# Feed-forward groups made of two sequence chunks of two batches, with a new emission order, in a fused linear-attention and SwiGLU kernel

## Chip, cores and metric

The kernel runs on one core of a Trainium2 chip. The metric is the device time of one execution in microseconds. A core has five engines with a queue of instructions each: TensorE (PE; its weight loads are shown as PEld), VectorE (DVE), ScalarE (ACT), GpSimd (POOL) and SyncE (SP), which here only issues DMAs. Engines run their own queues in order and wait for each other by semaphores.

## What is computed

Two steps follow each other. The first is a linear attention with a decaying state for 4 batches, 8 heads, a sequence of 768 and a head size of 48; the second is a root-mean-square norm and a SwiGLU feed-forward over the 3072 tokens with 384 features and 1536 hidden units.

```python
for t in range(S):
    cur = np.einsum('bhd,bhe->bhde', u[None] * kt, vt)
    y[:, :, t] = np.einsum('bhd,bhde->bhe', rt, state + cur)
    state = wt[:, :, :, None] * state + np.einsum('bhd,bhe->bhde', kt, vt)
...
xn = x / rms * rms_g
g = xn @ w_gate
silu = g * (1.0 / (1.0 + np.exp(-g)))
return silu * (xn @ w_val) @ w_out
```

Inputs and output are float32.

## The kernel before

The sequence is cut into six chunks of 128 positions. A unit of attention work is a chunk n of a batch j, written n.j. All 8 heads of one (n, j) are handled together: a tile has 128 positions in its partitions and 384 features. The state goes from chunk n to chunk n+1 of the same batch.

The attention of one (n, j) is a chain of small steps:

- load_r, load_k, load_v and load_w fetch the inputs, 192 KB each, from SyncE's queue. For chunks 0 and 1 one load_w.0.j fetches the decays of both (384 KB, L257); the others are at L244.
- ln (ScalarE) takes the logarithm of w; cs_mm (TensorE, L391 to L398) sums it along the chunk; exp_r and exp_k (ScalarE) turn the sums into factors; r_mul and k_mul multiply r and k by them (L440, L446); w_tot keeps the chunk's whole decay.
- rk_pe transposes both on TensorE (L469) and rk_tr copies the result out on ScalarE (L478); from chunk 2 on, rk_tr is a DMA transpose from SyncE's queue (L474).
- q_mm multiplies them (L487, L489), q_mask_e and q_mask_o apply the causal mask. For the odd heads VectorE does this (L502) in the pairs listed in ODD_DVE; otherwise ScalarE copies (q_copy_o) and GpSimd masks (L505).
- cast_v makes v bf16, on ScalarE for chunks 0 and 1 (L374). st_mm and st_new update the state (L515, L521, L522).
- bonus_mul (two GpSimd products, L452 and L453), bonus_sum (L457) and bonus_v (L462) make the term with u.
- y_mm (L532, L535) and x_add (L540) give the attention output. x_sq (L545), x_rstd and xn_mul (L558) norm it. For chunks 0 to 3, xn_pe transposes it on TensorE (L569) and xn_out writes it with the gain into the tile xnt (L580); for chunks 4 and 5, a DMA transpose (xn_tr, L563) and a gain on GpSimd (xn_gain, L586) do.

The feed-forward works on groups of 512 tokens. Group n has its own xnt tile of 384 features by 512 tokens. For each of 12 slices f of the hidden units, gate_mm.n.f and val_mm.n.f are three matmuls of 512 columns (L598), silu is on ScalarE (L231), h_mul on VectorE (L616). Then o_mm.n.j (L630) multiplies with the output weights, 12 matmuls for each of the four column blocks, o_out copies the result and out_dma stores it (L645). **Before, group n is chunk n of all four batches.**

The weights are loaded by GpSimd, which casts them: load_gv.g.h (L346) with h = 0 for gate and 1 for value, g = 0 for the slices f below 4 and g = 1 for the rest; load_wo (L352) for the output weights. Each stands at one place in GpSimd's order.

The order of the work is written out in ORDER, 1106 steps, and a loop at the end calls the function of each step, so that every engine's queue has its steps in that order. PSUM is shared out in the same order by three rings: "a" (two banks: cs_mm's sums, gate), "b" (two banks: the other sums, value) and "q" (four banks: all else). A step takes the bank whose last reader stands earliest. 48 steps warm.x.0 are matmuls on a tile of zeros whose result nobody reads (L369); they stand among the first steps.

Of the kernel before, what the change touches and what calls it, by code (L numbers as in the profile page):

```python
# [25 lines left out]
load_r.0.1 load_w.0.1 load_k.0.0 load_k.0.1 ln.0.1 warm.31.0 load_w.0.0 ln.0.0 warm.0.0 warm.13.0 warm.28.0  # L26
bonus_mul.0.1 bonus_sum.0.1 load_r.0.0 load_v.0.0 bonus_mul.0.0 load_w.0.2 load_w.0.3 warm.29.0 load_k.0.2 load_v.0.1
load_r.0.2 bonus_mul.0.2 load_r.0.3 load_v.0.3 load_v.0.2 bonus_v.0.1 load_r.1.3 load_k.1.0 cs_mm.0.1 exp_k.0.1
warm.10.0 warm.17.0 warm.33.0 warm.38.0 exp_r.0.1 r_mul.0.1 k_mul.0.1 bonus_sum.0.0 bonus_v.0.0 cs_mm.0.0 exp_r.0.0
ln.0.2 exp_k.0.0 cast_v.0.0 r_mul.0.0 k_mul.0.0 w_tot.0.0 warm.8.0 warm.16.0 warm.12.0 warm.4.0 warm.30.0 w_tot.0.1  # L30
rk_pe.0.1 warm.15.0 warm.14.0 load_k.0.3 bonus_mul.0.3 load_r.1.1 load_r.1.0 load_k.1.1 load_v.1.1 load_r.1.2 ln.0.3
load_k.1.3 warm.20.0 warm.37.0 warm.2.0 warm.22.0 warm.23.0 warm.5.0 warm.3.0 rk_pe.0.0 warm.24.0 load_gv.0.1
load_k.1.2 load_v.1.0 load_w.2.1 warm.25.0 load_v.1.2 load_w.2.0 load_v.1.3 load_r.2.1 load_r.2.0 load_w.2.2 warm.32.0
# [649 lines left out]
```

## Time and profile before

| | us |
|---|---|
| median of 3 runs | 203.21 (203.05 to 203.41) |
| span of the profiled execution, first to last instruction | 202.2 |
| median less that span | 1.0 |
| PE busy | 192.6 (95%) |
| PEld busy | 113.5 (56%) |
| DVE busy | 146.1 (72%) |
| ACT busy | 136.6 (68%) |
| POOL busy | 134.3 (66%) |
| first L598 matmul (val_mm.0.2) starts | 33.19 |
| last of the weight loads of gate (f of 4 and over) lands | 39.9 |
| last o_mm matmuls start | 198.1 |

The profiled execution's own time is known by its span alone; the 1.0 us between it and the median of the runs is what lies around it. "Busy" adds up the durations of an engine's instructions; matmuls overlap, so a TensorE that is busy all the time can still do its work faster or slower. The page also has a row for the TensorE clock that the throttle granted, full speed in all 40 slices. Idle time of an engine matters only where another, or the end, waits for it, and the chain of waits tells where that is.

### The profile page before, as it was taken

How to read it: one execution, taken by the hardware profiler on the slowest of the kernel's cores; microseconds unless marked ns; L12 is line 12 of the kernel's file. 1: busy time of each engine (PE TensorE's matmuls, PEld its weight loads, DVE VectorE, ACT ScalarE, POOL GpSimd, SP SyncE). 2: the span in 40 equal slices, each digit the busy share in tenths (PEclk: the TensorE clock that was granted, in tenths of full speed). 3: DMA queues.
4: the chain of work that ended last, by engine and by line, in shares of the span. 5: the costliest groups of instructions: out<-in, count | busy, mean ns of one | idle time of the engine just before them, and what ended most of it. 6: DMA issues, size and time to landing. Idle time of an engine off the chain costs nothing.

```text
span 202.2 us, 4444 instructions
## 1 busy us (share of the span) xinstructions
PE 192.6 (95%) x1600; PEld 113.5 (56%) x1600; DVE 146.1 (72%) x289; ACT 136.6 (68%) x278; POOL 134.3 (66%) x198
## 2 busy tenths in 40 slices
PE   1999988899999999999999999999999999999994
PEld 1564655455666555665556665555555555555562
DVE  6257796658999699987988889788878972146521
ACT  2577699688998557997566978679867764046300
POOL 6527599658789966899789898859898742400000
PEclk9999999999999999999999999999999999999999
DMA  6999999989999999958999978996184022103022
GB/s 152 243 244 177 209 182 202 202 161 201 199 192 221 196 179 238 225 133 194 177 231 245 206 171 195 216 241 134 24 192 112 15 68 71 45 3 117 0 97 99
DMA packets 121566, 32.41 MB, mean 160 GB/s; under 512 B 116420, under 2 KB 120392, under 8 KB 121544
## 3 DMA queue, kind: packets, MB, share of 16 engines
q1 hardware_dynamic: 119504, 28.58, 67.2%
q0 software_dynamic: 2032, 3.54, 9.7%
q8 instruction: 12, 0.20, 0.4%
q14 instruction: 10, 0.08, 0.1%
q10 hardware_dynamic: 8, 0.00, 0.0%
HBM read 25.96 MB, written 4.72 MB: 152 GB/s over the span
## 4 chain that ended last, share of the span: by engine, by line
PE 79%; SPq 8%; DMA 8%; POOL 2%; issue 1%; ACT 0%; POOLq 0%
PE ps_av L598 12%; PE ps_bu L598 12%; PE ps_bv L598 10%; PE ps_au L598 10%; PE ps_qx L630 8%; PE ps_qv L630 7%; SPq L244 7%; DMA wg_sb<-in_moe_w_gate_dram 6%; PE ps_qz L630 5%; PE ps_qu L630 3%; SPq L257 2%; DMA kt<-in_k_dram 2%; PE ps_qu L487 1%; PE ps_av L406 1%; PE ps_qu L515 1%
## 5 line engine op out<-in xcount | busy, mean ns | idle before, releaser
L630 PEld LDWEIGHTS <-ht 128*128 128x128 bf16 x300 | 28.3, 98 | 16.9
L231 ACT ACTIVATE sg<-ps_av 128x512 bf16<-128x512 f32 x38 | 22.7, 598 | 18.4 <-PE ps_av L598 16.8
L616 DVE TENSOR_TENSOR ht<-ps_bu,sg 128x512 bf16<-128x512 f32 x38 | 26.1, 686 | 11.7 <-PE ps_bu L598 8.4
L598 PEld LDWEIGHTS <-wg_sb 128*128 128x128 bf16 x216 | 22.8, 114 | 20.2 <-DMA wg_sb<-in_moe_w_gate_dram 2.1
L598 PEld LDWEIGHTS <-wv_sb 128*128 128x128 bf16 x216 | 23.2, 114 | 19.3 <-DVE xnt L580 0.2
L616 DVE TENSOR_TENSOR ht<-ps_bv,sg 128x512 bf16<-128x512 f32 x34 | 23.3, 686 | 12.2 <-PE ps_bv L598 8.8
L452 POOL TENSOR_TENSOR ruk<-rt,kt 128x384 f32<-128x384 f32 x24 | 24.0, 1000 | 11.1 <-DMA kt<-in_k_dram 6.0
L598 PE MATMUL ps_av<-xnt,wg_sb 128*128 128x512 bf16 x114 | 30.9, 380 | 0.4 <-DMA wg_sb<-in_moe_w_gate_dram 0.4
L231 ACT ACTIVATE sg<-ps_au 128x512 bf16<-128x512 f32 x34 | 20.4, 599 | 16.0 <-PE ps_au L598 14.6
L598 PE MATMUL ps_bu<-xnt,wv_sb 128*128 128x512 bf16 x114 | 30.9, 380 | 0.0
L598 PE MATMUL ps_au<-xnt,wg_sb 128*128 128x512 bf16 x102 | 27.7, 381 | 0.8 <-DMA wg_sb<-in_moe_w_gate_dram 0.8
L598 PE MATMUL ps_bv<-xnt,wv_sb 128*128 128x512 bf16 x102 | 27.7, 380 | 0.0
L453 POOL TENSOR_TENSOR ruk<-ruk,u_bc 128x384 f32<-128x384 f32 x24 | 23.9, 997 | 1.9
L462 POOL TENSOR_TENSOR ydiag<-vt,diag 128x384 f32<-128x384 f32 x24 | 19.7, 830 | 0.9 <-DVE diag L457 0.8
L446 POOL TENSOR_TENSOR rk<-kt,ek 128x384 bf16<-128x384 f32 x20 | 19.9, 1003 | 0.3 <-ACT ek L231 0.3
L505 POOL TENSOR_SCALAR_AFFINE_SELECT qts<-qts 128x512 bf16<-128x512 bf16 x20 | 12.5, 636 | 10.7 <-ACT qts L498 10.7
L630 PE MATMUL ps_qx<-wo_sb,ht 128*128 128x384 bf16 x96 | 16.9, 326 | 0.0
L630 PE MATMUL ps_qv<-wo_sb,ht 128*128 128x384 bf16 (+1 forms) x96 | 15.9, 316 | 0.0
L558 ACT ACTIVATE xn<-xb,rstd 128x384 bf16<-128x384 f32 x24 | 14.1, 608 | 1.2 <-POOL rstd L554 1.2
L457 DVE TENSOR_REDUCE diag<-ruk 128x8 f32<-128x384 f32 x24 | 12.9, 543 | 2.7 <-POOL ruk L453 2.7
L231 ACT ACTIVATE lw<-wt 128x384 bf16<-128x384 f32 (+1 forms) x20 | 11.2, 579 | 4.6 <-DMA wt<-in_w_dram 4.5
L229 ACT ACT_TABLE_LOAD x10 | 12.8, 1283 | 1.8 <-PEq L667 1.6
(153 smaller groups left out, 368.2 us busy)
## 6 DMA issues: line engine op xcount, KB each, us to landing
rt<-in_r_dram SPq DMA_DIRECT2D x24, 192.0 KB, 3.9
kt<-in_k_dram SPq DMA_DIRECT2D x24, 192.0 KB, 3.9
vt<-in_v_dram SPq DMA_DIRECT2D x24, 192.0 KB, 3.7
out_dram<-ob SPq DMA_DIRECT2D x23, 192.0 KB, 2.1
wt<-in_w_dram SPq DMA_DIRECT2D x16, 192.0 KB, 3.9
wt<-in_w_dram SPq DMA_DIRECT2D x4, 384.0 KB, 4.6
wo_sb<-in_moe_w_out_dram POOLq DMA_DIRECT2D x3, 384.0 KB, 5.2
wg_sb<-in_moe_w_gate_dram POOLq DMA_DIRECT2D x1, 768.0 KB, 12.0
```

The lines of the kernel that those rows point to most:

```text
L229: nc.scalar.preload_act_table_set(table_name)
L231: return nc.scalar.activation(**kw).ins
L244: dmas["load_" + which, n, j] = nc.sync.dma_start(out=inp[which, n, j], in_=t[j, :, n * L:(n + 1) * L, :].rearrange("h t d -> t h d")).ins
L446: eng.tensor_tensor(out=rk[:, n % 2, j, 1, :, 0:D], in0=inp["k", n, j], in1=bank["cs_k", n, j][:, 0:DM].rearrange("p (h d) -> p h d", h=H) ...
L452: nc.gpsimd.tensor_tensor(out=ruk[n, j], in0=inp["r", n, j], in1=inp["k", n, j], op=ALU.mult)
L453: nc.gpsimd.tensor_tensor(out=ruk[n, j], in0=ruk[n, j], in1=u_bc, op=ALU.mult)
L457: nc.vector.tensor_reduce(out=diag[n, j].rearrange("p h o -> p (h o)"), in_=ruk[n, j], axis=mybir.AxisListType.X, op=ALU.add)
L462: nc.gpsimd.tensor_tensor(out=ydiag[n, j], in0=inp["v", n, j], in1=diag[n, j].to_broadcast([128, H, D]), op=ALU.mult)
L558: nc.scalar.activation(out=xn, in_=xb[n, j], func=AF.Copy, scale=rstd[n, j][:, 1:2])
L598: nc.tensor.matmul(ps, lhsT=units(ws, c, f), rhs=xnt[n][:, c, :], start=(c == 0), stop=(c == KC - 1))
L616: nc.vector.tensor_tensor(out=ht[n][:, f, :], in0=bank.pop(("v", n, f)), in1=bank.pop(("sg", n, f)), op=ALU.mult)
L630: nc.tensor.matmul(ps[:, cols], lhsT=ht[n][:, f, b * L:(b + 1) * L], rhs=wo_sb[:, f, cols], start=(f == 0), stop=(f == FC - 1))
```

## The change

The number of feed-forward groups and their size stay. Groups 0 and 1 get other columns: group 0 is chunks 0 and 1 of batches 0 and 1, group 1 chunks 0 and 1 of batches 2 and 3. COL maps an (n, j) to its group and column block, CHUNK maps back; x_cols gives the part of xnt to write, out_dma takes the rows from CHUNK. Groups 2 to 5 are as before. The four (n, j) whose k_mul, q_mask_o and x_rstd are on VectorE or ScalarE change with the groups: K_POOL, EXPK_SB, ODD_DVE and RSTD_ACT now list 0.0, 0.1, 1.0 and 1.1 where 0.0 to 0.3 stood, so q_copy_o.0.2 and q_copy_o.0.3 are there and q_copy_o.1.0 and q_copy_o.1.1 are not. xn_gain loses a branch that no step took. The rest of ORDER, to the last step, is written anew; it has the same number of steps. Its core, and the rest of the diff:

```diff
 ORDER = """
-load_r.0.1 load_w.0.1 load_k.0.0 load_k.0.1 ln.0.1 warm.31.0 load_w.0.0 ln.0.0 warm.0.0 warm.13.0 warm.28.0
-bonus_mul.0.1 bonus_sum.0.1 load_r.0.0 load_v.0.0 bonus_mul.0.0 load_w.0.2 load_w.0.3 warm.29.0 load_k.0.2 load_v.0.1
-load_r.0.2 bonus_mul.0.2 load_r.0.3 load_v.0.3 load_v.0.2 bonus_v.0.1 load_r.1.3 load_k.1.0 cs_mm.0.1 exp_k.0.1
-warm.10.0 warm.17.0 warm.33.0 warm.38.0 exp_r.0.1 r_mul.0.1 k_mul.0.1 bonus_sum.0.0 bonus_v.0.0 cs_mm.0.0 exp_r.0.0
-ln.0.2 exp_k.0.0 cast_v.0.0 r_mul.0.0 k_mul.0.0 w_tot.0.0 warm.8.0 warm.16.0 warm.12.0 warm.4.0 warm.30.0 w_tot.0.1
-rk_pe.0.1 warm.15.0 warm.14.0 load_k.0.3 bonus_mul.0.3 load_r.1.1 load_r.1.0 load_k.1.1 load_v.1.1 load_r.1.2 ln.0.3
...
-xn_mul.0.3 exp_k.1.3 xn_pe.0.3 r_mul.1.3 xn_out.0.3 cast_v.1.1 k_mul.1.1 load_gv.1.1 rk_pe.1.1 st_mm.1.1 exp_k.1.2
-exp_r.1.2 w_tot.1.2 r_mul.1.2 w_tot.1.3 bonus_mul.1.3 val_mm.0.2 val_mm.0.3 warm.46.0 gate_mm.0.2 gate_mm.0.3 rk_tr.1.1
-q_mm.1.1 silu.0.2 h_mul.0.2 load_k.2.0 silu.0.3 h_mul.0.3 bonus_sum.1.3 st_new.1.1 gate_mm.0.0 val_mm.0.1 rk_tr.1.0
-bonus_mul.1.0 val_mm.0.0 load_r.2.3 silu.0.0 q_mask_e.1.1 h_mul.0.0 bonus_mul.1.1 bonus_sum.1.1 gate_mm.0.6 silu.0.6
-gate_mm.0.1 silu.0.1 q_mm.1.0 q_copy_o.1.0 gate_mm.0.5 silu.0.5 h_mul.0.1 q_mask_e.1.0 bonus_sum.1.0 gate_mm.0.7
...
-gate_mm.4.10 silu.4.10 val_mm.4.10 h_mul.4.10 val_mm.4.11 h_mul.4.11 o_mm.4.1 o_mm.4.0 o_mm.4.2 x_rstd.5.2 xn_mul.5.2
-x_rstd.5.3 xn_mul.5.3 xn_tr.5.3 xn_tr.5.2 xn_gain.5.2 xn_gain.5.3 out_dma.3.3 xn_gain.5.1 o_mm.4.3 gate_mm.5.5 silu.5.5
-o_out.4.2 val_mm.5.5 gate_mm.5.2 h_mul.5.5 val_mm.5.2 gate_mm.5.1 silu.5.2 h_mul.5.2 silu.5.1 gate_mm.5.7 silu.5.7
...
+load_w.0.0 load_r.0.1 load_k.0.0 load_v.0.0 ln.0.0 warm.43.0 warm.24.0 warm.27.0 warm.20.0 warm.17.0 warm.25.0
+load_w.0.3 load_r.0.0 warm.9.0 warm.28.0 warm.22.0 warm.16.0 warm.30.0 warm.7.0 warm.34.0 warm.31.0 warm.5.0
+load_k.0.1 warm.19.0 warm.29.0 warm.42.0 warm.11.0 warm.15.0 warm.37.0 warm.47.0 warm.14.0 warm.39.0 cast_v.0.0
+load_w.0.1 ln.0.1 ln.0.3 warm.8.0 load_v.0.1 load_v.1.1 cast_v.1.1 warm.38.0 load_w.0.2 warm.13.0 warm.36.0 load_v.0.3
+load_r.1.1 load_k.1.1 ln.0.2 bonus_mul.0.1 bonus_sum.0.1 bonus_v.0.1 bonus_mul.0.0 warm.35.0 warm.21.0 warm.4.0
+warm.45.0 warm.46.0 warm.44.0 warm.0.0 warm.26.0 warm.32.0 warm.18.0 warm.6.0 warm.3.0 warm.10.0 warm.23.0 warm.12.0
+warm.33.0 bonus_sum.0.0 cast_v.0.1 cs_mm.0.1 warm.2.0 exp_r.0.1 cs_mm.0.0 exp_k.0.1 load_v.1.0 r_mul.0.1 exp_k.0.0
+k_mul.0.1 w_tot.0.1 k_mul.0.0 warm.41.0 warm.40.0 warm.1.0 rk_pe.0.1 exp_r.0.0 st_mm.0.1 st_mm.0.0 r_mul.0.0 w_tot.0.0
...
+k_mul.1.1 r_mul.1.1 rk_pe.1.1 q_mask_o.0.0 w_tot.1.1 load_k.1.3 load_k.1.2 load_k.0.2 load_r.0.2 load_gv.0.1
+bonus_v.0.0 cast_v.1.0 rk_tr.1.0 q_mm.1.0 exp_r.0.3 rk_tr.1.1 exp_k.0.3 cs_mm.0.2 exp_r.0.2 x_sq.0.1 q_mask_e.0.0
+q_mask_e.1.0 q_mask_o.1.0 y_mm.0.0 x_add.0.0 load_r.1.2 q_mm.1.1 load_v.0.2 q_mask_e.1.1 bonus_sum.1.0 q_mask_o.1.1
+w_tot.0.2 r_mul.0.3 x_sq.0.0 x_rstd.0.1 st_mm.1.0 y_mm.1.0 st_mm.1.1 load_v.1.3 load_v.1.2 load_gv.0.0 bonus_mul.0.3
+bonus_v.1.1 bonus_v.1.0 x_rstd.0.0 xn_mul.0.1 xn_mul.0.0 exp_k.0.2 y_mm.1.1 k_mul.0.3 w_tot.0.3 x_add.1.1 x_sq.1.1
+load_gv.1.0 k_mul.0.2 bonus_mul.0.2 x_add.1.0 load_w.2.0 load_w.2.1 xn_pe.0.1 load_r.2.0 load_w.2.2 load_r.2.1
...
+xn_mul.1.1 cs_mm.1.2 xn_pe.1.1 xn_mul.1.0 xn_pe.1.0 xn_out.1.1 exp_r.1.3 exp_k.1.2 exp_r.1.2 exp_k.1.3 xn_out.1.0
+rk_pe.0.2 st_mm.0.3 r_mul.1.3 w_tot.1.2 rk_tr.0.3 val_mm.0.2 st_new.0.3 k_mul.1.3 load_gv.1.1 k_mul.1.2 bonus_mul.1.3
+r_mul.1.2 w_tot.1.3 val_mm.0.3 st_new.1.1 gate_mm.0.3 silu.0.3 gate_mm.0.2 silu.0.2 q_mm.0.3 rk_pe.1.3 h_mul.0.3
+gate_mm.0.1 q_copy_o.0.3 cast_v.0.2 gate_mm.0.0 st_mm.0.2 val_mm.0.1 rk_tr.0.2 bonus_sum.0.3 q_mask_e.0.3 h_mul.0.2
+bonus_v.0.3 silu.0.1 silu.0.0 q_mm.0.2 val_mm.0.0 q_copy_o.0.2 bonus_sum.0.2 q_mask_o.0.2 gate_mm.0.5 bonus_v.0.2
+h_mul.0.1 q_mask_e.0.2 gate_mm.0.6 y_mm.0.2 silu.0.5 q_mask_o.0.3 gate_mm.0.7 st_new.0.2 h_mul.0.0 silu.0.6 silu.0.7
...
+silu.4.10 out_dma.3.3 xn_tr.5.0 xn_tr.5.1 x_sq.5.2 xn_mul.5.3 x_rstd.5.2 xn_mul.5.2 xn_tr.5.3 xn_gain.5.0 xn_tr.5.2
+val_mm.4.10 xn_gain.5.1 xn_gain.5.3 h_mul.4.10 h_mul.4.11 o_mm.4.1 o_mm.4.0 xn_gain.5.2 o_mm.4.2 out_dma.3.0
+out_dma.3.2 val_mm.5.2 gate_mm.5.2 gate_mm.5.8 val_mm.5.8 silu.5.2 silu.5.8 h_mul.5.2 gate_mm.5.1 silu.5.1 val_mm.5.1
...
 """
...
@@ -177,8 +178,8 @@
 
     CAST_ACT = sel("00 01 02 03 10 11 12 13")
     EXPR_SB = sel("")
-    K_POOL = sel("10 11 12 13 20 21 22 23 30 31 32 33 40 41 42 43 50 51 52 53")
-    EXPK_SB = sel("10 11 12 13") | K_POOL
+    K_POOL = sel("02 03 12 13 20 21 22 23 30 31 32 33 40 41 42 43 50 51 52 53")
+    EXPK_SB = sel("10 11") | K_POOL
     WIN = (0, 1)
     Q_PAIR = ((2, 0), (2, 2), (3, 0), (3, 2), (4, 0), (4, 2), (5, 0), (5, 2))
     OLD_DVE = (1, 2, 3, 4)
@@ -187,9 +188,15 @@
     GAIN_POOL = (4, 5)
     RK_PE = sel("00 01 02 03 10 11 12 13")
     RK_DVE = sel("")
-    ODD_DVE = sel("00 01 02 03")
-    RSTD_ACT = sel("00 01 02 03")
+    ODD_DVE = sel("00 01 10 11")
+    RSTD_ACT = sel("00 01 10 11")
     OUT_DVE = sel("00 02 10 12 20 22 30 32 40 42 50 52 53")
+
+    COL = {(0, 2): (1, 0), (0, 3): (1, 1), (1, 0): (0, 2), (1, 1): (0, 3)}
+    CHUNK = {v: k for k, v in COL.items()}
+
+    def col_of(n, j):
+        return COL.get((n, j), (n, j))
 
     def banks_of(fn, n, j):
         if fn == "q_mm":
@@ -337,7 +344,7 @@
     FG = 4
     wg_sb = [persist.tile([128, KC, (b - a) * 128], BF16, name="wg_sb%d" % a) for a, b in zip(GV, GV[1:])]
     wv_sb = [persist.tile([128, KC, (b - a) * 128], BF16, name="wv_sb%d" % a) for a, b in zip(GV, GV[1:])]
-    GV_BEHIND = (None, None)
+    GV_BEHIND = (None, None, None)
     WO_BEHIND = (None, None, None)
 
     def load_gv(g, h):
@@ -557,10 +564,14 @@
         xn = bank["xn", n, j] = pt.tile([128, DM], BF16, name="xn", bufs=3)
         nc.scalar.activation(out=xn, in_=xb[n, j], func=AF.Copy, scale=rstd[n, j][:, 1:2])
 
+    def x_cols(n, j):
+        g, c = col_of(n, j)
+        if g not in xnt:
+            xnt[g] = pt.tile([128, KC * TS], BF16, name="xnt")
+        return xnt[g].rearrange("p (c x) -> p c x", c=KC)[:, :, c * L:(c + 1) * L]
+
     def xn_tr(n, j):
-        if n not in xnt:
-            xnt[n] = pt.tile([128, KC, TS], BF16, name="xnt")
-        nc.sync.dma_start_transpose(xnt[n][:, :, j * L:(j + 1) * L], bank.pop(("xn", n, j)))
+        nc.sync.dma_start_transpose(x_cols(n, j), bank.pop(("xn", n, j)))
 
     def xn_pe(n, j):
         ps = bank["xt", n, j] = psum("q", ("xt", n, j), [128, KC, 128], BF16)
@@ -569,24 +580,19 @@
             nc.tensor.transpose(ps[:, c, :], xn[:, c * 128:(c + 1) * 128], ident)
 
     def xn_out(n, j):
-        if n not in xnt:
-            xnt[n] = pt.tile([128, KC, TS], BF16, name="xnt")
+        x_t = x_cols(n, j)
         ps = bank.pop(("xt", n, j))
         if (n, j) in XOUT_ACT:
             for c in range(KC):
-                nc.scalar.activation(out=xnt[n][:, c, j * L:(j + 1) * L], in_=ps[:, c, :], func=AF.Copy,
+                nc.scalar.activation(out=x_t[:, c, :], in_=ps[:, c, :], func=AF.Copy,
                                      scale=gT[:, c:c + 1])
         else:
-            nc.vector.tensor_tensor(out=xnt[n][:, :, j * L:(j + 1) * L], in0=ps,
+            nc.vector.tensor_tensor(out=x_t, in0=ps,
                                     in1=gT.to_broadcast([128, KC, L]), op=ALU.mult)
 
     def xn_gain(n, c):
-        if n in GAIN_POOL:
-            x = xnt[n][:, :, c * L:(c + 1) * L]
-            nc.gpsimd.tensor_tensor(out=x, in0=x, in1=gT.to_broadcast([128, KC, L]), op=ALU.mult)
-        else:
-            nc.vector.tensor_scalar(out=xnt[n][:, c, :], in0=xnt[n][:, c, :], scalar1=gT[:, c:c + 1],
-                                    scalar2=None, op0=ALU.mult)
+        x = x_cols(*CHUNK.get((n, c), (n, c)))
+        nc.gpsimd.tensor_tensor(out=x, in0=x, in1=gT.to_broadcast([128, KC, L]), op=ALU.mult)
 
     def units(ws, c, f):
         g = max(i for i, x in enumerate(GV) if x <= f)
@@ -595,7 +601,7 @@
 
     def fc_mm(ps, ws, n, f):
         for c in range(KC):
-            nc.tensor.matmul(ps, lhsT=units(ws, c, f), rhs=xnt[n][:, c, :],
+            nc.tensor.matmul(ps, lhsT=units(ws, c, f), rhs=xnt[n].rearrange("p (c x) -> p c x", c=KC)[:, c, :],
                              start=(c == 0), stop=(c == KC - 1))
 
     def gate_mm(n, f):
@@ -640,9 +646,11 @@
         bank["ob", n, j] = ob
 
     def out_dma(n, j):
+        ob = ("ob", n, j)
         b, cols = out_cols(n, j)
-        row0 = b * S + n * L
-        nc.sync.dma_start(out=out[row0:row0 + L, cols], in_=bank.pop(("ob", n, j))[:, cols])
+        i, j = CHUNK.get((n, b), (n, b))
+        row0 = j * S + i * L
+        nc.sync.dma_start(out=out[row0:row0 + L, cols], in_=bank.pop(ob)[:, cols])
 
 
     fns = locals()
```

## The prediction

> **What bounds the kernel now.** I read the page's summary, then the chain of waits that ended last, then its pieces in order of time. By engine the chain is nearly all TensorE:
>
> ```profile
> PE 79%; SPq 8%; DMA 8%; POOL 2%; issue 1%; ACT 0%; POOLq 0%
> ```
>
> The 21% that are not TensorE all lie ahead of 39.9 us. The chain in order of time (start, duration, what; the loads on SyncE's queue come before it):
>
> ```profile
> 18.64 3.76 DMA kt<-in_k_dram
> 22.47 1.00 POOL ruk L452
> 24.49 0.99 POOL wv_sb L346
> 26.34 0.78 issue
> 27.12 0.78 POOL ydiag L462
> 27.90 11.95 DMA wg_sb<-in_moe_w_gate_dram
> 39.90 0.84 PE ps_av L598 x3
> ```
>
> So: the loads, one after another; the last load of chunk 0 (k of batch 3) lands at 22.4; GpSimd makes the bonus product of it, and only then issues the weight loads that stand behind it in its order; the third of them, the gate weights for f of 4 and over, lands at 39.9. From there TensorE has no hole. The busy times by stretch (PE in the second column of figures) say the same:
>
> ```profile
> 30.00:35.00 5.00, 4.81 (x52) 2.94 (x50) 3.79 (x10) 4.95 (x13) 4.82 (x6) 1.00 1.21 206
> 35.00:40.00 5.00, 3.98 (x24) 1.88 (x25) 2.82 (x6) 3.54 (x5) 3.48 (x4) 1.00 1.13 201
> 40.00:45.00 5.00, 5.00 (x42) 2.91 (x43) 3.41 (x7) 3.63 (x7) 2.41 (x4) 1.00 0.90 172
> 80.00:90.00 10.00, 10.00 (x97) 6.33 (x94) 9.97 (x21) 9.19 (x22) 8.18 (x14) 1.00 0.84 187
> ```
>
> I checked it by counting. Matmul spacings from the timeline, warm clock: a gate or value unit 0.648 us, an o_mm 1.95 (the halves 0.99), cs_mm of the window 0.84, later 0.26 and 0.16, rk_pe 0.45, q_mm 0.33 a chunk, st_mm 0.165, xn_pe 0.165, y_mm 0.2 for chunk 0 and 0.4 later. Over the whole order this is 177 us. Ahead of gate_mm.0.6 (39.90) stand 17.9, behind it 159.4, and the last matmul ends about 199.3: 199.3 - 39.9 = 159.4. **After 39.9 there is nothing to win**, only to lose; ahead of it 39.9 us hold 17.9 us of work.
>
> **The sum's frame.** The new order has the same matmuls. Its time is 203.2 plus what the dense stretch starts later or earlier (each measured after crediting the work already done), plus new holes. The span was 202.2, the median of the runs 203.21; I put the 1.0 between them around the span, in both kernels.
>
> **Loads.** Counted in KB in SyncE's order, the last load that the first four chains need is number 18 in both: load_k.0.3 before, load_r.1.0 now, each at 4224 KB in all (the four 384 KB w loads are still among the first eleven). The queue never paused up to there (the pieces on it abut from 0.80 to 19.6 us), so load_r.1.0 lands at 22.4 too. The saving that the grouping allows, two w loads of 384 KB, isn't taken.
>
> **Warm matmuls.** 44 of the 48 now stand ahead of the first cs_mm, five before. They are spaced 0.32 us until 11.4 and 0.163 after: 17 of them from 5.94, then 27 x 0.163 = 4.4, so cs_mm.0.1 starts at about 15.8 instead of 7.5. Its w is the 2112th KB, whose Ln ran at 11.8 before, so some 3 us are lost to them. Covered: both chunks' cs_mm are through by about 22, when the load for r_mul.1.0 lands; if that cover goes, up to 1 us.
>
> **GpSimd up to the first unit.** From 22.47: bonus_mul.1.0 2.0, load_gv.0.1 at 24.5, bonus_v.0.0, load_gv.0.0 at 26.3, all as before. Then, where before one bonus_v (0.78) ended at 27.9, now come bonus_mul.0.3 (2.0), bonus_v.1.1 and bonus_v.1.0 (0.8 each): end 27.1 + 3.6 = 30.7, **2.8 later**. VectorE's own work is ready then (q_mask_o.1.1 about 29.0). The last x_add before started at 28.73, the first unit at 33.19: 4.46 of x_sq, rstd, xn_mul, transpose, xn_out. Now x_add.1.0 at 30.8 gives the first unit at 35.3.
>
> **From there to the dense stretch.** Ahead of gate_mm.0.5, the first that needs the late gate weights, stand 8 units 5.2, two q_mm 0.66, rk_pe 0.45, st_mm 0.17: 6.5, so 41.8; ScalarE's chain (four Exp 1.55, rkT copy 0.92, table load 1.28, Silu 0.52 each, from 34.2) lets it go at 42.0. Before, 39.90 with 17.9 us of work done; now 19.9 done (one rk_pe, q_mm, st_mm and unit more, and two y_mm of chunk 1 in place of chunk 0's). Even would be 41.9. **+0.1 to +0.2.**
>
> **Weight loads.** load_gv.1.0 is issued at 31.7 instead of 27.9, load_gv.1.1 at 36.7 instead of 30.6, behind k_mul and bonus_mul. Before, they landed one behind another at 32.0, 35.6, 39.9, 44.1. The third needs 4.3 after the second, so issued at 31.7 it lands at 39.9 to 41, the fourth at 44 to 45.5, and their first users are at 42.0 and 46.5. Cost 0; without that cover up to 1.
>
> **A wait that is new.** st_mm.0.2 stands in TensorE's order ahead of val_mm.0.1 and needs cast_v.0.2, hence load_v.0.2, load 26, at 5760 KB. Load 26 before (v of chunk 1, batch 0) was starved:
>
> ```profile
> 25.64 1.30 SPq L244 DMA_DIRECT2D vt<-in_v_dram  x1
> ```
>
> It took 15.1 us and landed at 40.7. The reason, in the DMA view from 36 to 38 us (packets, MB, share of the engines):
>
> ```profile
> q0 software_dynamic: 193, 0.37, 97.1%
> q1 hardware_dynamic: 195, 0.04, 16.4%
> ```
>
> Packets of the weight queue and of SyncE's queue alternate one for one, and a weight packet is some ten times as large. Behind the waiting cast_v.0.2 on ScalarE are rk_tr.0.2 and two Silu; on TensorE val, q_mm, val and gate. ScalarE reaches the cast at 39.5. At 40.7 the whole goes 1.1 later; with a landing before 39.5 it is free. GpSimd issues the third weight load 3.8 later, and from issue to first packets took some 2 us (24.5 to between 26 and 28), so SyncE's packets get a pause between the second and third: I take a landing near 38.6, cost 0: midway between 40.7 and the 36.6 at which SyncE's packets, summed over the DMA views, reached 5760 KB before.
>
> **Groups 1 to 4.** From the last y_mm of a group to its first unit TensorE has 11.2, 10.7, 14.0, 10.2 us of other work, before 10.9, 10.7, 7.8, 9.7: no worse. VectorE, ScalarE and GpSimd have as much work in all (k_mul, q_mask_o and rstd change chunks, not number), so I put 0.
>
> **Group 5.** Before, the first unit comes after all four o_mm of group 4; now after three. The cover from y_mm.5.2 to the first unit falls from 13.4 to 10.8. It was thin:
>
> ```profile
> 172.85 2.39 POOL L586 TENSOR_TENSOR xnt<-xnt,gT 128x384 bf16<-128x384 bf16 x3 [4.56 <-DMA xnt<-xn]
> ```
>
> The last gain ends at 175.24, the unit starts at 175.75. The new chain is shorter, for x_add.5.2 waits for one h_mul: x_add at 1.4 after y_mm.5.2 starts, second x_sq done at 4.95, rstd 5.8, xn_mul 6.4, the second transpose issued at 6.8, landed 2.7 to 3.7 later, gain 0.83: 10.3 to 11.4 against 10.8. I take **+0.6**; ends 0 and 2.1 (the old chain's length under the new cover).
>
> The x_cols views, the output rows and the unused third entry of GV_BEHIND add no instruction: 0, both ways.
>
> **Sum:** 203.2 + 0.2 + 0.6 = **204.0**.
>
> **Rivals.**
> *Earlier (faster), 202.5.* The place is x_add.1.0. If GpSimd's and VectorE's pieces overlap better than I laid them and the first unit starts at 34.4 or before, gate_mm.0.5 runs at 41.0, 0.9 ahead of even, with group 5 late by 0.2. It decides at 35.2 for the first unit. For it: the weights themselves land by 39.9 to 41. Against: GpSimd's order is fixed behind a load that lands at 22.4. 0.22.
> *The v wait bites, 205.1.* The 40.7 row as it stands: +1.1. 0.16.
> *Group 5 waits in full, or q_mm waits for transposes behind loads on SyncE's queue, 205.5.* The old chain under the new cover: 203.2 + 0.2 + 2.1. Against: the shorter steps above. 0.14.
> *The slow matmul spacing returns, 206.5.* These are two warm matmuls and the rate they started from:
>
> ```profile
> 9.97 0.52 PE L369 MATMUL ps_qx<-zero 128*128 128x384 bf16 x1
> ...
> 11.40 0.32 PE L369 MATMUL ps_qz<-zero 128*128 128x384 bf16 x1
> 11.56 0.33 PE L369 MATMUL ps_qu<-zero 128*128 128x384 bf16 x1
> ```
>
> It took 5.4 us of steady matmuls to halve the spacing. With warm matmuls gone after 18 us, TensorE works some 3.6 of the 5.8 us from 29.5 to 35.3; were it slowed again, the first 5.4 us of units would lose half, 2.7, less 0.2 hidden by the weights' landing. Against: no hole over about 1 us by my reckoning. 0.10. The Trainium skill ("TensorE: Matmul & The Clock Gate", What's actually happening and Part 4: PE-mode transpose) halves the clock after an idle window of about 3.4 us and doesn't count transposes as busy in the same way. That speaks against this order, for by my reckoning only transposes run from 33.0 to 35.3; but 2.3 us are less than that window, so by the rule the time stays at the forecast. No trace here shows the clock fall back.
>
> **Chances.** Forecast 0.38, the rivals as given. About 0.2% (0.4 us) is what a measurement can tell from no change. Faster 0.22; same 0.14 (the lower part of the forecast); slower 0.64. Range 202.3 to 206.0: it leaves out the slowest rival and the far end of the first.
>
> **What would show it.** The first L598 matmul at 35.3 (33.2 before); first use of the late gate weights near 42.0; cast_v.0.2 not waiting for its load; a hole under 1 us ahead of group 5's first unit; none elsewhere after 42. It is wrong if the first unit comes before 34.5, if spacings of 0.43 us (twice 0.216) for 128x512 matmuls appear, or if waits appear in groups 1 to 4.

## The result and the profile after

The changed kernel takes **209.13 us** (median of 4 runs, 207.81 to 210.28), the kernel before 203.13 beside it: a ratio of 1.028 (1.023 to 1.034), 6 us slower. (Ratios are the record's own estimate and can differ a little from that of two medians; they leave out the longest run of three kernels further down, a2, w1 and w3, which the record counts as slow.) The forecast was 204.0, the range 202.3 to 206.0. The profiled execution is the 207.81 one, with a span of 206.1 us.

The chain by engine, where before had 79% TensorE:

```profile
PE 57%; SPq 12%; POOL 11%; DMA 7%; ACT 5%; issue 3%; DVE 2%; POOLq 0%; DVEq 0%; ACTq 0%
```

The chain now leaves TensorE in the middle of the kernel. There are three kinds of loss.

**Holes.** A hole here is the time from one matmul's start to the next beyond its streaming, counted from 0.25 us up (the profile's idle time is some 0.15 shorter, for it ends at the modelled end). Behind the first feed-forward group before had none. The changed kernel has 0.26 at 92.16, 0.56 at 126.88, 0.27 at 129.81, 1.48 at 135.38, 0.52 at 153.00: **3.1 us**. (One more, 0.31 at 47.22, lies in its first group and is counted with the start.) The largest two, from TensorE's timeline (start, duration, engine, line, tile; in brackets the idle time and what ended it):

```profile
126.88 0.23 PE L494 MATMUL ps_qx<-rkT 48*128 48x128 bf16 x1 [0.39 <-DMA rkT<-rk]
...
135.38 0.23 PE L494 MATMUL ps_qz<-rkT 48*128 48x128 bf16 x1 [1.32 <-DMA rkT<-rk]
```

Both are q_mm of chunk 4, waiting for a transpose from SyncE's queue. The one at 153.00 is the first unit of group 4, waiting for the gain that GpSimd applies behind the last transpose of its tile.

**A sparse start.** TensorE's timeline some microseconds ahead of the first unit:

```profile
27.82 0.33 PE L522 MATMUL ps_qv<-vb,rk 128*128 128x96 bf16 x4
28.88 0.33 PE L539 MATMUL ps_qu<-st,rkT 128*128 128x96 bf16 x4 [0.73 <-DVE qts L509]
29.04 0.36 PE L542 MATMUL ps_qu<-vb,qts 128*128 128x48 bf16 x8
30.73 0.33 PE L580 MATMUL ps_qu<-ident,xn 128*128 128x128 bf16 x3 [1.33 <-DVE xb L547]
```

From 28.0 to 30.7 it does 0.4 us of work. In this execution that costs nothing: the clock stays up, the first unit starts at 35.25 and the first late gate weights are used at 41.93. In three of the four runs the mean granted clock is 0.989 to 0.991 instead of 1.000, and they take 209.03 to 210.28. The experiments show what happens there.

**The ends.** Time less span is 1.7 us in every run of both kernels (207.81 less 206.1); from the last matmul's end to the span's end it is 3.3 us, before 2.95.

### The profile page after: what moved, and what is told of

Its sections match the earlier page's. It is cut to its first block, busy times and chain, and to the rows that moved or that the text cites. A ratio compares the mean times of both kernels' runs of the same rounds, so it can differ in the third digit from the quotient of the medians.

```text
span 206.1 us, 4427 instructions
## 1 busy us (share of the span) xinstructions
PE 191.3 (93%) x1580; PEld 114.2 (55%) x1600; DVE 146.0 (71%) x289; ACT 136.9 (66%) x278; POOL 135.1 (66%) x198
## 3 DMA queue, kind: packets, MB, share of 16 engines
HBM read 25.96 MB, written 4.72 MB: 149 GB/s over the span
## 4 chain that ended last, share of the span: by engine, by line
PE 57%; SPq 12%; POOL 11%; DMA 7%; ACT 5%; issue 3%; DVE 2%; POOLq 0%; DVEq 0%; ACTq 0%
PE ps_av L604 10%; PE ps_bv L604 10%; SPq L251 9%; PE ps_au L604 8%; PE ps_bu L604 8%; PE ps_qz L636 4%; PE ps_qx L636 4%; PE ps_qu L636 4%; PE ps_qv L636 3%; SPq L264 3%; POOL ruk L459 2%; POOL ruk L460 2%; DMA rkT<-rk 2%; DMA kt<-in_k_dram 2%; DMA wt<-in_w_dram 2%
## 5 line engine op out<-in xcount | busy, mean ns | idle before, releaser
L622 DVE TENSOR_TENSOR ht<-ps_bv,sg 128x512 bf16<-128x512 f32 x39 | 26.8, 687 | 20.2 <-PE ps_bv L604 11.1
L238 ACT ACTIVATE sg<-ps_av 128x512 bf16<-128x512 f32 x39 | 23.4, 599 | 21.4 <-PE ps_av L604 17.6
L604 PE MATMUL ps_bv<-xnt,wv_sb 128*128 128x512 bf16 x109 | 31.0, 380 | 0.3
L238 ACT ACTIVATE sg<-ps_au 128x512 bf16<-128x512 f32 x33 | 19.8, 600 | 13.3 <-PE ps_au L604 9.2
L622 DVE TENSOR_TENSOR ht<-ps_bu,sg 128x512 bf16<-128x512 f32 x33 | 22.7, 688 | 8.4 <-PE ps_bu L604 5.2
L604 PE MATMUL ps_bu<-xnt,wv_sb 128*128 128x512 bf16 x95 | 26.4, 380 | 0.5 <-POOL xnt L595 0.4
L604 PE MATMUL ps_au<-xnt,wg_sb 128*128 128x512 bf16 x95 | 26.3, 380 | 0.3
L460 POOL TENSOR_TENSOR ruk<-ruk,u_bc 128x384 f32<-128x384 f32 x24 | 24.4, 1015 | 1.9
L636 PE MATMUL ps_qu<-wo_sb,ht 128*128 128x384 bf16 x96 | 16.9, 326 | 0.0
L552 ACT ACTIVATE junk<-xb 128x384 bf16<-128x384 f32 x24 | 12.5, 521 | 1.2 <-DVE xb L547 1.0
```

The costliest lines, as they stand in the source:

```text
L238: return nc.scalar.activation(**kw).ins
L460: nc.gpsimd.tensor_tensor(out=ruk[n, j], in0=ruk[n, j], in1=u_bc, op=ALU.mult)
L604: nc.tensor.matmul(ps, lhsT=units(ws, c, f), rhs=xnt[n].rearrange("p (c x) -> p c x", c=KC)[:, c, :], start=(c == 0), stop=(c == KC - 1))
L622: nc.vector.tensor_tensor(out=ht[n][:, f, :], in0=bank.pop(("v", n, f)), in1=bank.pop(("sg", n, f)), op=ALU.mult)
L636: nc.tensor.matmul(ps[:, cols], lhsT=ht[n][:, f, b * L:(b + 1) * L], rhs=wo_sb[:, f, cols], start=(f == 0), stop=(f == FC - 1))
```

## The experiments

All kernels in one table, but for x1 and y1, which come under "The queue". "Clock held": runs with a mean granted clock of 0.998 or more. (One stretch of 3.41 us at half speed takes 0.008 off the mean, so the 0.997 of one run each of w3 and e2 is less than one such stretch. The profiles of e1 and z1 hold no clock record; there the spacing of the matmuls shows no fall.) The profile's columns: its run's time, the start of the first unit, the holes behind the first group, and the "rest", the end of the last matmul less the holes; it shows what the start costs, for the matmuls of the groups are the same. Ratios are to the kernel before, with their 95% interval.

| kernel | median, us | ratio | clock held | run | first unit | holes | rest |
|---|---|---|---|---|---|---|---|
| before | 203.1 | | all | | 33.19 | 0 | 199.3 |
| before, again | 204.00 | | 1 of 1 | 204.00 | 33.57 | 0.9 | 198.5 |
| changed | 209.13 | 1.028 (1.023 to 1.034) | 1 of 4 | 207.81 | 35.25 | 3.1 | 199.7 |
| changed, again | 209.79 | 1.034 (1.028 to 1.040) | 1 of 4 | 209.85 | 37.26 | 3.2 | 201.6 |
| changed, third | 210.74 | 1.034 (1.029 to 1.039) | 0 of 6 | 211.21 | 38.16 | 3.7 | 202.4 |
| e1 transposes first | 208.31 | 1.025 (1.018 to 1.032) | 3 of 4 | 206.80 | 35.91 | 1.6 | 200.5 |
| h1 new start, old rest | 208.26 | 1.025 (1.018 to 1.032) | 1 of 4 | 206.69 | 35.47 | 1.4 | 200.2 |
| h2 old start, new rest | 209.80 | 1.034 (1.028 to 1.040) | 0 of 4 | 209.84 | 33.66 | 4.4 | 200.8 |
| w1 filled | 208.67 | 1.027 (1.024 to 1.031) | 5 of 6 | 208.05 | 36.09 | 2.5 | 200.5 |
| w2 fewer first warms | 209.46 | 1.031 (1.028 to 1.034) | 0 of 6 | 209.06 | 36.77 | 2.8 | 201.2 |
| w3 both | 211.15 | 1.035 (1.030 to 1.040) | 2 of 6 | 211.25 | 37.72 | 3.9 | 202.3 |
| w4 h1, filled | 207.52 | 1.021 (1.018 to 1.024) | 5 of 5 | 207.76 | 36.75 | 1.4 | 201.3 |
| w5 h1, fill in one bank | 206.67 | 1.019 (1.017 to 1.021) | 4 of 4 | 206.49 | 35.19 | 1.7 | 199.7 |
| w6 changed, fill in one bank | 206.11 | 1.016 (1.012 to 1.019) | 6 of 6 | 207.61 | 35.97 | 2.3 | 200.3 |
| e2 w6, loads behind | 205.76 | 1.016 (1.013 to 1.018) | 5 of 6 | 205.48 | 35.36 | 0.7 | 199.7 |
| z2 e2, more loads behind | 207.73 | 1.022 (1.019 to 1.026) | 6 of 6 | 207.57 | 35.78 | 2.1 | 200.5 |
| z1 before, loads behind | 206.69 | 1.017 (1.013 to 1.022) | 4 of 6 | 206.25 | 33.71 | 3.1 | 198.5 |
| b2 before, fewer late warms | 203.35 | 1.000 (0.998 to 1.003) | 1 of 12 | 202.01 | 32.62 | 0 | 197.3 |

### Which half, and does it repeat

Four kernels ran first: the changed kernel unedited (a1); e1, with the transposes of chunk 4 ahead in SyncE's queue; and two mixed orders, cut at the first unit of group 2.

```diff
 e1:
-... rk_tr.4.0 out_dma.2.1 out_dma.1.3 load_v.4.2 rk_tr.4.1 load_v.4.3 load_v.5.3 ... rk_tr.4.3 rk_tr.4.2
+... rk_tr.4.0 rk_tr.4.1 out_dma.2.1 out_dma.1.3 load_v.4.2 load_v.4.3 rk_tr.4.3 rk_tr.4.2 load_v.5.3 ...
 h1: changed order up to gate_mm.2.5, then the steps that are left in before's order
 h2: before's order and code up to val_mm.2.1, then the steps that are left in the changed order
```

> The changed kernel once more, unedited. Theory (order): its loss is in waits that come back in every run, so the holes of TensorE at q_mm.4.0 (0.56 us) and q_mm.4.2 (1.48 us) are there again and the ratio to before is 1.025 to 1.032. Rival (clock): three of its four runs had a mean granted clock of 0.989 to 0.991 and were 1.2 to 2.5 us longer than the profiled one, which had 1.000; by this rival a profile with 0.99 shows a stretch of about 4 us at half speed somewhere after the first matmuls, with 128x512 matmuls 0.43 us apart, and the extra 1.2 to 2.5 us lie there.

> The changed kernel with rk_tr.4.1 ahead of the two stores and the load that stood before it on SyncE's queue, and rk_tr.4.3, rk_tr.4.2 ahead of load_v.5.3, out_dma.2.2, load_w.5.2 and load_r.5.2. Theory (SyncE's order): the transposes for q_mm.4.0 and q_mm.4.2 land 1.7 and some 4 us earlier, both holes go, the time falls by 1.5 to 2.1 us, more if the clock fell because of the holes. Rival (GpSimd's order): k_mul.4.2, which ends at 126.6, holds the second transpose, and the hole at q_mm.4.2 shrinks by less than half; the time falls by 0.6 to 1.0.

> The changed kernel's steps up to the first unit of group 2, so the new groups 0 and 1 and their order, then all steps that are left in the order of the kernel before. Theory (the late order costs, the regrouping doesn't): 203.0 to 203.8, no hole after 42 us. Rival (regrouping costs: by its sparse stretch before 35 us the clock falls): 205 or more, with a mean clock of 0.99 and no holes in groups 4 and 5.

> The reverse: the kernel before, old groups and old order, up to the first unit of group 2, then all steps that are left in the changed kernel's order. Theory (the late order costs): 206.5 to 209, with the holes at q_mm.4.0 and q_mm.4.2. Rival (regrouping and the early order cost): 203.0 to 205.2, holes of at most 2 us in all and a mean clock of 0.999.

Measured: **a1** repeats the loss and shows the clock. The stretches of its profile and of the second profile of before (us from the start, length, then busy time of TensorE, its weight loads, VectorE, ScalarE, GpSimd; granted clock, DMA share, GB/s), a1 first:

```profile
28.00:31.70 3.70, 1.49 (x30) 1.28 (x30) 2.85 (x8) 3.03 (x12) 3.60 (x6) 1.00 1.15 183
31.70:35.10 3.40, 3.40 (x28) 2.38 (x27) 2.98 (x6) 3.11 (x11) 3.38 (x5) 0.50 1.21 205
```

```profile
28.00:31.70 3.70, 3.59 (x55) 2.77 (x54) 3.60 (x10) 3.60 (x13) 3.02 (x5) 1.00 1.22 198
```

The clock is halved from 31.71 to 35.12, just when the transposes and sums ahead of the first unit run. In the stretch before it TensorE was busy for 1.49 us; in before it was busy for 3.59 in the same stretch. Two matmuls of cs_mm, in the changed kernel's first profile and in a1:

```profile
30.90 0.49 PE L398 MATMUL ps_au<-lw,mw 128*128 128x384 bf16 x2
```

```profile
31.79 0.85 PE L398 MATMUL ps_au<-lw,mw 128*128 128x384 bf16 x2
```

The first unit comes at 37.26, not 35.25, though the GpSimd chain that feeds it ends at the same time in both (30.96 and 30.89). **e1**'s hole of 1.48 is gone; 0.43 and 0.94 came at q_mm.4.0, where o_out waited for a buffer whose store now stands behind the transposes. So the queue's order makes such holes, but this edit only moves them: 1.6 us are left of 3.1. Its median is 1.5 us under a1's; as its clock held in three of four runs and a1's in one, how much of that is the holes is not shown. **h1**: my theory that the late half carries the loss fell, 208.26 against 203.0 to 203.8 expected; but its holes halved. **h2** has one hole of 3.72 us behind its seam, in which the clock fell too; it says little of the changed order.

### The clock

The zero matmuls called warm are the only part of the start that can be changed freely. w1 adds 12 in the sparse stretch, w2 takes 14 of the first 44 away, w3 does both; b1 is before, unedited.

```diff
 w1:
-        ps = psum("q", ("warm", n, j), [128, DM])
+        ps = psum("b" if j else "q", ("warm", n, j), [128, DM])
-... st_mm.1.1 load_v.1.3 ... exp_k.0.2 y_mm.1.1 k_mul.0.3 ...
+... st_mm.1.1 warm.0.1 ... warm.3.1 load_v.1.3 ... exp_k.0.2 y_mm.1.1 warm.4.1 ... warm.11.1 k_mul.0.3 ...
 w2: the last 14 warm steps ahead of cs_mm.0.1 are taken out
```

> The kernel before, unedited, for a profile of a second execution. My forecast set 1.0 us around the span; every later run of either kernel showed 1.7 (time less span). If 1.7 is the constant, the profiled execution of before (span 202.2) was one of the longer ones, and this one shows a span of 200.7 to 201.8 for a time of 202.5 to 203.5, with its first late gate unit (f of 4 and over) well ahead of 39.9, at about 39.0, for the same work behind it (159.4 us to the last matmul). Rival: 1.0 was right for that execution; then the first late gate unit is again at 39.7 to 40.1 and the difference lies behind it.

> The changed kernel with 4 more zero matmuls behind the state matmuls of 1.1 and 8 more behind the y matmuls of 1.1, where TensorE idled from 28.0 to 28.9 and from 29.2 to 30.7. The sum isn't changed by them (nobody reads them). Theory A (the granted clock falls to half for 3.4 us in most executions because TensorE is sparse there, and that delays the first units): mean granted clock 0.999 or more in at least three of four runs in place of one of four, less spread between runs, and the median 0.8 to 1.2 us lower than the changed kernel's, about 208.1. Rival B (the fall costs nothing, since the weights or the normed tile end last there): clocks rise all the same, the time stays within 0.4 us of 209.1 to 209.8. Rival C (the fall isn't set by this stretch): the clocks stay at 0.99.

> The changed kernel without 14 of the 44 zero matmuls ahead of the first cumulative sum. In the changed kernel's profile that sum starts at 14.58, while its input was ready at 12.74 (ScalarE's logarithm of 11.90 lasts 0.84); in the profile where the clock rose at 11.23 instead of 8.95 it starts at 15.69. Theory A (the row of warm matmuls stands on the chain to the first unit): the first sum at 12.8 to 13.4, the first unit 1 to 2 us earlier, and the time 1 to 2 us lower (207.5 to 208.5). Rival B (a later input, the normed tile's weights or GpSimd's chain ends last): first sum earlier, first unit within 0.3 us, time within 0.4 us of 209.1 to 209.8.

> Both edits of the start together. If theory A holds for both, they add: 1.8 to 3 us lower than the changed kernel, 206.5 to 207.5, and what is left over the kernel before (203.1) is the 3.4 us of holes of TensorE behind 90 us and 0.4 us of the tail. If the start costs nothing (rival), 209 to 209.8 again.

**b1** took 204.0 with a span of 202.3: 1.7 around the span. Both profiled executions of before are among the long ones (its spans run from 200.3 to 202.9). The first late gate unit is at 39.00, as expected, 0.9 ahead of the other execution, and 0.9 us of holes at the q_mm of chunks 3 and 4 give it back. **w1**: the clock held in 5 of 6 runs, the gain was only 0.5 to 2.1 us, by which of the three medians of the changed kernel it is set against. **w2** was no gain: the first sum came at 13.30 instead of 14.58, but the clock fell in all six runs, in the profiled one at 30.95, where the unedited order loses it too. **w3** took 211.15, not the 206.5 to 207.5 expected: the sum came at 12.95, and the clock fell at 19.02 already, for from 15.3 to 18.0 the warm row had run out and nothing else was ready. Here the missing warm matmuls cost the clock: with the same fill, w1 held it in 5 of 6 runs and w3 in 2 of 6.

w4, the mixed order h1 with the same fill, shows why the fill gained so little. Its TensorE timeline (eight filling matmuls, the first two shown, then the first transpose of the normed tile):

> The changed kernel's first steps, up to the first unit of group 2, with the 12 zero matmuls in its sparse stretch, and the order of before behind them. If the two causes add (a clock that falls in the start, 3 us of holes of the late order): clocks 0.999 or more in most runs, holes of 1 to 1.7 us as in the mixed order without the fill, and 206.0 to 207.0, about 2 us under the changed kernel. What then is left over before (203.3) is what the new start itself costs: 2.7 to 3.7. Rival (the fall costs nothing): 208 to 208.5 again, as the mixed order had without the fill (208.26).

```profile
30.82 0.32 PE L377 MATMUL ps_bu<-zero 128*128 128x384 bf16 x1
31.34 0.32 PE L377 MATMUL ps_bv<-zero 128*128 128x384 bf16 x1 [0.20 <-ACT ek L239]
...
32.64 0.33 PE L581 MATMUL ps_qu<-ident,xn 128*128 128x128 bf16 x3
```

207.52, all runs within 0.6 us of each other. The filling matmuls waited for a bank that ScalarE's exponential still read, and the transpose, which runs at 30.73 in the changed kernel's first profile and at 31.60 in a1, stood behind them until 32.64. w5 (h1) and w6 (the changed kernel) write the fill into one free bank:

```diff
...
-        ps = psum("q", ("warm", n, j), [128, DM])
+        if j and "fill" not in bank:
+            bank["fill"] = psum("b", ("fill", 0, 0), [128, DM])
+        ps = bank["fill"] if j else psum("q", ("warm", n, j), [128, DM])
```

> As the run with the filled start and the old order behind it (207.52), but all 12 filling matmuls write one PSUM bank that has long been read. In that run's profile they took turns with a bank that ScalarE's exponential of k read until 31.30, so eight of them ran at 31.34 to 32.7 and the first transpose of the normed tile, which started at 30.7 to 31.0 in the changed kernel, came at 32.64. Theory A (the start is a chain through that transpose): it starts at 30.7 to 31.3 (31.5 where the clock rises late), clocks 0.999 or more, and the time is 1.0 to 1.6 us lower, 205.9 to 206.5. Rival B (the groups after it wait for something else, so that the 1.6 us were hidden): 207.2 to 207.8 again.

> The changed kernel itself with that fill. Theory A: clocks 0.999 or more, the time 207.0 to 207.8, about 1.5 us under the changed kernel as it stands (209.1 and 209.8) and 1.2 to 1.8 over the mixed order of the same call, the price of the late order. Rival B: as the first fill, 208.67, or higher.

**w5** 206.67, **w6** 206.11, clock held in all ten runs. Twelve matmuls that compute nothing make the changed kernel 3 to 4.6 us faster (209.13, 209.79 and 210.74 without them, each beside a before of the same time within 0.3 us); by the ratios it is 1.3 to 1.8%. Not all of that is shown to be the clock. The two runs in which the unedited kernel held it took 207.81 and 209.22, its twelve others 208.15 to 212.31; w6's six, all held, took 205.12 to 207.61, and the profiled one, 207.61, is no shorter than the changed kernel's 207.81. What else the fill changes is open. The late order, which theory A priced at 1.2 to 1.8 us over the mixed one, costs nothing over it here (w6 is 0.6 us below w5): the seam of h1 makes a hole of its own, in w5 1.41 us at 96.75. The last two runs on the clock are the changed kernel a third time and the mirror, before without 21 of its late warm matmuls:

> The changed kernel, unedited, once more beside the next two on one chip. If the fall of the granted clock belongs to its order and not to a chip or a moment: mean clock 0.984 to 0.992 in most of its runs, median 208.5 to 210. Rival: the clocks are 1.0 here and the time is 206 to 207.5 as with the fill.

> The mirror of the fill: the kernel before without the last 21 of its 48 zero matmuls, those that run behind 17 us between the attention steps. Worked out from before's profile (384 columns are 0.163 us of TensorE): with them no stretch of 3.41 us holds less than 51% of matmul work; without them every stretch that starts between 16.6 and 25.8 us has some that hold under 38%, down to 13%. Theory A (the clock falls in such a stretch, whatever the order): mean granted clock 0.983 to 0.992 in all or nearly all runs, where before has 1.0. What that costs is open: if the matmuls between 19 and 32 us stand on the chain, 0.5 to 2 us (203.7 to 205.2); if the weights' landing near 39.9 covers them, less than 0.3. Rival B (the fall belongs to the changed order): clock 1.0, time as before.

**a2**: the clock fell in all six runs, in the profiled one twice in a row, from 30.91 to 37.74, and the first unit came at 38.16. **b2**: the clock fell in 11 of 12 runs, so the spread of warm matmuls, and not the grouping, is what keeps before's clock up. It cost nothing, ratio 1.000 (0.998 to 1.003). Two stretches of its profile at half clock and its chain show why:

```profile
20.10:23.50 3.40, 3.40 (x40) 2.17 (x37) 2.81 (x6) 2.73 (x8) 1.57 (x2) 0.51 1.08 213
...
27.00:30.40 3.40, 3.17 (x31) 2.49 (x32) 2.89 (x9) 3.30 (x12) 3.38 (x5) 0.50 1.19 208
```

```profile
26.50 0.78 POOL ydiag L461
27.27 10.64 DMA wg_sb<-in_moe_w_gate_dram
37.91 0.05 issue
37.96 0.84 PE ps_av L597 x3
```

The falls lie ahead of 30.4, and the late gate weights, which land at 37.9, cover them. In a1 and a2 they lie between 31 and 38, on the way to the first units, and no later load covers them: in a1 the late gate weights, issued at 32.6, land 8.7 us later at the latest, by 41.3, and are first used at 43.95.

### The queue

Swapping the whole of SyncE's queue between the kernels, from the first store to the transposes of chunk 4, was meant to part the queue's order from the computation's:

> The changed kernel, every instruction of the computing engines in its own order; only SyncE's queue, from the first store to the transposes of chunk 4 of batches 2 and 3, goes in the order that the kernel before has (71 DMAs; 13 places differ from it, where the changed computation needs another order). Theory A (the late holes are made by what stands ahead of the transposes in SyncE's queue): TensorE's holes behind 90 us fall from about 3.3 us to 1.5 or less, and the time to 206.5 to 207.5. Rival B (the order of the computation makes them): holes of 2.5 to 4 us, the time 208.5 to 210.

> The mirror of it: the kernel before, its computing engines and its start untouched; only SyncE's queue from the second load of v of chunk 2 to the transposes of chunk 4 goes in the changed kernel's order (65 places). Theory A: holes like those of the changed kernel, 2 to 3 us more than before, 205.3 to 206.3. Rival B: no more holes than before has (0 to 1.2 us), 203.0 to 204.0.

226.95 (ratio 1.116, 1.112 to 1.120) and 235.34 (1.157, 1.152 to 1.161), with 16 and 26 us of holes. Each order of the queue fitted only its own order of the computation; this told nothing of the cause. A smaller edit did, six loads of chunk 5 moved behind the transposes of chunk 4, on top of w6:

```diff
-... load_r.5.1 ... load_v.5.0 ... load_w.5.0 ... load_v.5.3 out_dma.2.2 load_w.5.2 load_r.5.2 rk_tr.4.3 rk_tr.4.2
+... out_dma.2.2 rk_tr.4.3 rk_tr.4.2 load_r.5.1 load_v.5.0 load_w.5.0 load_v.5.3 load_w.5.2 load_r.5.2
```

> The run before it, with six loads of chunk 5 (r.5.1, v.5.0, w.5.0, v.5.3, w.5.2, r.5.2) moved in SyncE's queue from ahead of the transposes of chunk 4 to right behind the last of them; transposes and stores keep their order. Theory A (what stands ahead of the transposes in that queue makes the holes at q_mm of chunk 4): the holes of TensorE between 125 and 140 us, 1.4 to 2.3 in the changed kernel's profiles, fall below 0.7, and the time by 0.7 to 1.6 us under the unmoved order. Rival B (the transposes wait for GpSimd's and VectorE's products anyway, so that the queue hides nothing): holes and time as without the move, within 0.3 us. Rival C: the moved loads are late for chunk 5, new holes behind 150 us.

SyncE's queue in the changed kernel, then in e2:

```profile
124.78 1.35 SPq L251 DMA_DIRECT2D vt<-in_v_dram  x2
126.23 1.34 SPq L653 DMA_DIRECT2D out_dram<-ob  x1
127.62 0.43 SPq L264 DMA_DIRECT2D wt<-in_w_dram  x1
128.10 0.72 SPq L251 DMA_DIRECT2D rt<-in_r_dram  x1
128.93 2.06 SPq L481 DMA_TRANSPOSE rkT<-rk  x1
```

```profile
125.09 0.36 SPq L658 DMA_DIRECT2D out_dram<-ob  x1
125.56 2.77 SPq L486 DMA_TRANSPOSE rkT<-rk  x2
128.39 0.58 SPq L254 DMA_DIRECT2D rt<-in_r_dram  x1
```

GpSimd's products for the two transposes ended at 123.2 and 126.6 in the changed kernel; they were issued at 128.9 and 131.1, behind two loads of v, a store and two more loads. In e2 the first goes at 125.56, and TensorE has no hole from 124 to 137. Its busy times from 125 to 140 in the changed kernel, then in e2 (first engine figure of a line):

```profile
125.00:132.00 7.00, 6.44 (x56) 3.52 (x56) 6.07 (x12) 3.85 (x10) 5.67 (x9) 1.00 1.09 213
132.00:140.00 8.00, 6.62 (x58) 3.74 (x58) 4.78 (x9) 4.94 (x11) 4.57 (x9) 1.00 0.80 114
```

```profile
125.00:132.00 7.00, 7.00 (x61) 3.90 (x59) 6.81 (x13) 4.68 (x12) 6.92 (x10) 1.00 0.96 208
132.00:140.00 8.00, 8.00 (x78) 4.72 (x77) 5.58 (x11) 5.79 (x13) 5.41 (x11) 1.00 0.88 177
```

Against w6, the run it was edited from, the holes of the profile fall from 2.3 to 0.7 us and its time from 207.61 to 205.48. Only 0.8 of those 1.6 us were at the q_mm of chunk 4 (0.44 and 0.39, both gone); the rest is a smaller hole at the q_mm of chunk 3 (1.19 to 0.45), which the edit doesn't touch. The medians, 206.11 and 205.76, differ by less than their spread (205.1 to 207.6), so the mechanism is shown, its mean price isn't.

The same idea once more, on e2 (z2: r.4.0, w.5.3, w.4.1, k.4.2, k.5.3 behind the last transposes of chunk 3) and on before (z1: four loads behind those of chunk 3, five behind those of chunk 4):

> The changed kernel with the fill in one bank, the six loads of chunk 5 behind the transposes of chunk 4, and five more loads (r.4.0, w.5.3, w.4.1, k.4.2, k.5.3) moved from ahead of the last transposes of chunk 3 to behind them. Theory A (loads ahead of the transposes in SyncE's queue make the holes): the hole at q_mm of chunk 3, 0.45 to 1.2 in the profiles so far, falls under 0.3, and the time to 204.8 to 205.6 from 205.76. Rival B (that hole is the transposes' own time): 205.5 to 206.2, the hole as it was. In both cases slower than before (202.9), by what the new start and the tail cost.

> The kernel before with the same idea: k.4.1, k.5.3, r.4.2, r.4.1 from ahead of the last transposes of chunk 3 to behind them, and k.5.2, r.5.2, k.5.1, w.5.0, k.5.0 from ahead of the transposes of chunk 4 to behind them. One profiled execution of before had no hole, the other 0.52 and 0.35 us at the q_mm of chunks 3 and 4. Theory A: those go where they occur, the time falls by 0.2 to 0.8 us, 202.2 to 202.8. Rival B: the transposes themselves (4.1 us from issue to landing) make them, within 0.2 us of before. Rival C: the moved loads land late, slower.

Both lost: 207.73 and 206.69. GpSimd now waited for a load, in z2:

```profile
113.40 4.69 DMA rt<-in_r_dram
118.16 1.01 POOL ruk L464
```

GpSimd's bonus product of that load is due there, and z1 has the like at 128.34 (4.72 us). A load that is moved behind a transpose is free only if its reader comes later still. No version beat before.

## Why the prediction was wrong, point by point

Right, in the profiled execution: the **landing of the loads and GpSimd's chain** (end 30.7 forecast, 30.88 found; weight loads issued at 24.57, 26.38, 31.78, 36.63 against 24.5, 26.3, 31.7, 36.7); the **first unit** (35.3; 35.25); the **late gate weights** (42.0; 41.93); the **v wait**, which cost nothing (ScalarE reached cast_v.0.2 at 39.26); the first sum's delay by the **warm row** (15.8 forecast; 14.58, and 15.69 in a1, by the moment at which the clock rises). **Group 5**, +0.6 forecast, had no hole; a wait of just that kind, for the gain, came ahead of group 4's first unit instead (0.52).

Wrong, with what each is worth in the profiled execution:

- **"Groups 1 to 4 ... I put 0"**: 3.1 us of holes in place of 0.6 (+2.5). I counted each engine's work and TensorE's cover, and didn't lay SyncE's queue beside them. I had the case only as half of a rival, for group 5, at 205.5.
- **"I put the 1.0 between them around the span"**: it is 1.7 (+0.7). The median of other runs less one execution's span isn't what lies around a span; that execution was a long one.
- **The tail** wasn't in the sum: +0.4. I did not look for its cause.
- **The start**, +0.2 forecast: 199.7 against 199.3, +0.2 more. Against before's other execution, 198.5, it costs 1.2.

204.0 + 2.5 + 0.7 + 0.4 + 0.2 = 207.8, the time of that execution. The three other runs took 1.2 to 2.5 us more. That goes with the rival **"The slow matmul spacing returns"**, to which I gave 0.10: their mean clocks are 0.989 to 0.991, and in a1, with 0.992, the fall moves the first unit by 2.0 us. (Runs with the clock held differ among themselves too, by 2.5 us in w6.) The rival named the right stretch; the fall lasted 3.41 us, or twice that, and hit the transposes and sums ahead of the first unit, where I had put 5.4 us of units. The step that failed is "no hole over about 1 us by my reckoning": I laid out 29.5 to 35.3 as working 3.6 us, and missed that from 28.0 to 30.7 hardly anything runs. I treated the 44 warm matmuls as a row in the way and asked only what the row delays, not what the 21 of them that ran behind 17 us had done before: keep the clock up. In the four profiles with the new start and a fall in it (a1, a2, w2, w3) the rest is 201.2 to 202.4 us; in the nine with the clock held it is 199.7 to 200.5, save w4 with its delayed transpose (201.3). "No trace here shows the clock fall back" was a misreading as well: in before's own trace the clock falls at 201.96, 2.7 us behind the end of the last matmul, and the page's 40 slices were too coarse to show it.

Open: what sets the size of the holes from one execution to the next (3.1, 3.2 and 3.7 in the changed kernel, 0 and 0.9 in before); why e1, with an untouched start, kept the clock in 3 of 4 runs, beyond the place of the windows; and the remaining 3 us of e2 over before, of which the profiles name 0.4 to 1.2 us of start, 0.7 of holes, 0.4 of tail; and what else the fill gained than the clock.

## What to carry to other kernels

Matmuls that compute nothing belong to a schedule like any other step: before moving them, ask over every stretch of 3.4 us how much TensorE still works without them. When an order is written anew, lay the DMA queue beside the engines, item by item: a transpose is as late as the store or load ahead of it, and a load moved out of the way must still meet its own reader. And make the sum against the same execution's time, not the median of others.

## What the runs showed of the hardware

The clock goes by a fixed grid of windows: it rose between 8.8 and 12.0 us, by the execution, and each fall came a whole number of 3.41 us later (31.71 is 11.23 and 6 windows) and lasted one to three windows. As an estimate, I counted the matmuls' streaming time (0.163 us for 384 columns, transposes included) in the windows of the 18 profiles that have a clock record, x1 and y1 among them: the 13 windows behind which the clock fell, up to the last matmul, held 0 to 44%; those behind which it stayed held 45% or more, but for one (38%). Where matmuls that run side by side count once, it is 0 to 38% against 41% or more, but for the same one. Before's order holds at least 51% in any 3.41 us from 13 us on; the changed order, in its first profile, less than 38% in each that starts between 26.5 and 28.4, so whether its clock falls depends on where the grid lies. The length agrees with the Trainium skill ("TensorE: Matmul & The Clock Gate", What's actually happening: a free-running window of 3413 ns), but its condition, an idle window, doesn't: here 38% of work wasn't enough. Nor are transposes, which stand in these traces as matmuls with an identity tile, left out as in its Part 4: PE-mode transpose: in w5 the window from 31.39 held 28% without and 62% with them, and the clock stayed.
